# Attention, Fourier mixing and a feed-forward block in one kernel: instruction order from a table, and two PSUM tiles for the last product

## The chip, the cores and the metric

The kernel runs on one core of one Trainium2 chip. A core has TensorE (PE in the profile: matrix products, written to PSUM), VectorE (DVE), ScalarE (ACT), GpSimd (POOL) and SyncE (SP); each engine runs its own queue of instructions in the order in which they were put there, and waits on semaphores for the others. POOL and SP issue the transfers as well. The metric is the device time of one execution in microseconds (us); lower is better. Three executions of the kernel before took 565.71, 566.06 and 567.05 us, median 566.06.

## The reference

Inputs are `q`, `k`, `v` of (8, 12, 448, 64) and the weights `w_ch1` (768, 3072) and `w_ch2` (3072, 768); the output is (8, 448, 768), float32.

```python
scores = np.matmul(q, k.transpose(0, 1, 3, 2)) / np.sqrt(64)
attn = np.maximum(scores, 0.0) ** 2 / 448
x = np.matmul(attn, v).transpose(0, 2, 1, 3).reshape(8, 448, 768)
X = np.fft.fft(np.fft.fft(x, axis=1), axis=2)
u = x + np.real(X)
un = (u - mean(u)) / np.sqrt(var(u) + 1e-06)      # over the last axis
out = u + np.maximum(un @ w_ch1, 0.0) @ w_ch2
```

## The kernel before

Everything is bf16 on TensorE. The work is cut into pieces that are Python generators ("streams"); each `yield need(engine, duration, deps, bufs)` asks for one step on one engine, and emits the step's instructions when it is let on. `Streams.run` is a list scheduler that runs while the program is built: it keeps an estimated clock for each engine, and lets on the stream that can begin first, with small head starts by kind of stream and phase. So the order on every queue comes out of estimated durations. Nothing of this runs on the chip.

The streams, with the lines that show in the profile:

- **Loading** (POOL's queue, `load_group` L478, `load_halves` L453): q, k and v of one batch and four heads at a time. From batch 2 on DVE rearranges q and k (L585) and SP turns them by DMA (L595); batches 0 and 1 are turned on PE (L625).
- **Attention**: 21 items for each batch. An item's scores are two products (L956, PSUM tiles `psS`, three of them with two banks each, `BS`); ACT applies the relu (L969), which frees the PSUM tile, and DVE squares in place (L986; some squares are on ACT, L983). Six times a batch four squared items meet `v` (L824, L829, PSUM tile `psF`, two banks, `BF`), and the result leaves to `xT` (L691 on DVE, L688 on ACT).
- **Mixing**: `x` is folded by symmetry on DVE (L762 to L782), meets the channel table (L1434) and the sequence table (L1242, L1246); L1254 to L1259 take the two halves of PSUM apart. `mix_rows` adds `x` (L1277, L1279: one half of the rows on DVE, the other on POOL), takes the statistics (L1286, L1287 on DVE, root L1289 on ACT, L1291, L1292 on DVE), and normalises (L1305 on ACT or L1302 on POOL). `un` goes to DRAM (L1340, L1343) and comes back turned (L1382); batches 0 and 1 are turned on PE (L1132, L1207).
- **Feed-forward** over 12 groups of tokens, the last four of 256 tokens in two pairs. First products L1934 into `psF`, relu into `hT` on ACT (L1921) or DVE (L1919). The second products run as plain sums (L1962), or as two schemes that save products by sums of blocks: `whole` (L1989) and `Pair` (L2075). A scheme adds one PSUM tile to two blocks of the output, so that a product into a tile can go on only when DVE has added the tile as it is so far to its block `o` (L1625); then the tile goes on accumulating. In `joint`, the last two pairs, the first products are saved in the same manner: L1766, with copies of the running sums on ACT (L1781).
- **Output**: `o` starts as `u` from DRAM (L1597), and is stored when all its additions are in (L1605, SP's queue).
- **Warming** (L2158): 252-column products of zeros that fill PE's queue in the head of the program until the first batch's channel mixing is through.

`Pair.chain_a` is a tile's chain of four products: block by block it is added to `(c, 0)`, `(c+1, 0)`, `(c+1, 1)` and, complete, to `(c, 1)`. In the very last pair the fourth product is done in two halves of 192 columns, `parts`, both into the chain's own tile, so that the first half of the rows can be added and stored apart.

Of the kernel before, what the change touches and what calls it, by code (L numbers as in the profile page):

```python
# [41 lines left out]
class Banks(Bufs):  # L42
# [6 lines left out]
    def take(self, apart=None):  # L49
        first = min(self.ids)  # L50
        if apart is not None:
            held = {i // 2 for _, i in self.tiles.values() if i < 6}
            first = min(self.ids, key=lambda x: (x[0] > apart, x[1] // 2 in held, x))
        self.ids.remove(first)
        t = self.make(first[1])
        self.tiles[id(t)] = t, first[1]
        return t
# [7 lines left out]
HEAD = {('attentions', 'PE', 2): -0.6, ('attentions', 'PE', 3): -0.6, ('attentions', 'PE', 4): 0.07, ('mix_rows', 'PE', 2): -0.05}  # L65
# [3 lines left out]
PHASES = (48.0, 140.0, 290.0, 440.0)  # L69


class Streams:
# [29 lines left out]
    def run(self):  # L102
        end = {}
        while self.streams:
            for s in self.streams:
                if s[2] is None:
                    try:
                        s[2] = s[0].send(end.pop(id(s), None))
                    except StopIteration:
                        s[2] = ()  # L110
            self.streams = [s for s in self.streams if s[2] != ()]
            best = spare = None
            now = self.engine["PE"]
            phase = sum(now >= x for x in PHASES)
            for s in self.streams:
                eng, dur, deps, bufs, ok = s[2]
                if any(isinstance(d, Cell) and d.t is None for d in deps):
                    continue
                if any(len(p.free) < bufs.count(p) for p in bufs):
                    continue  # L120
                t = [self.engine[eng]] + [d.t if isinstance(d, Cell) else d for d in deps]
                for p in set(bufs):
                    t.append(sorted(p.free)[bufs.count(p) - 1])
# [3 lines left out]
                if key[0] and eng == "PE" and self.fill() and (spare is None or key < spare[0]):  # L127
                    spare = (key, s)
            if best is None:
                assert not self.streams, "stuck"  # L130
                break
            if best[1][2][0] == "PE" and spare is not None and best[0][1] - spare[0][1] > 0.5:
                best = spare
# [12 lines left out]
            end[id(s)] = start + dur  # L146
            s[2] = None

# [29 lines left out]
def kernel(  # L178
# [63 lines left out]
    STAGE[0] = 1  # L242
# [406 lines left out]
    def fold(b, m, F, av, give, av_end):  # L649
# [4 lines left out]
        def leave():  # L654
# [10 lines left out]
            if b == 0:  # L665
                bufs = [BX[m]] + ([BA[m]] if m < 3 else [])
                wait = {x: max(av_end, sch.engine[x]) + sch.queued(x) for x in ("ACT", "DVE")}
                en = "ACT" if m == MC - 1 or m in (3, 4) and wait["ACT"] + 2 * act(HS) < wait["DVE"] + 2 * dve(HS) else "DVE"
# [167 lines left out]
    def attention(b, left=None):  # L836
# [8 lines left out]
        while pv < MC:  # L845
            if p == NB and pv == MC - 1 and 2 <= b < B - 1 and turned_at[b + 1][0][0].t is not None:
                return F, sqs
            few = b == 0 or progress[0] == 0.0
# [15 lines left out]
            if values:  # L864
                deps += [sv[i][1] for i in items(mv)]
                if b > 1:
                    yield need("PE", 0.0, deps, [], gate)
                    if chains[0] == 2:
                        homes, n = BS, min(n, 2)
# [92 lines left out]
    def squares(b, scs, sqs):  # L962
        for i, sc, t in scs:
            e = yield need("ACT", act(2 * S) - (0.0 if STAGE[0] else 0.03), [t + LATENCY["PE"]], [BSQ])
            at = min(sq_ids)
            sq_ids.remove(at)
# [8 lines left out]
    def sooner(t, other, d, usual, du):  # L975

        wait = {en: max(t, sch.engine[en]) + sch.queued(en) for en in (other, usual)}
        return wait[other] + d + SPARE < wait[usual] + du
# [637 lines left out]
    def adder(b, NC, pool):  # L1616
# [4 lines left out]
        def add(pc, e, c, hf, give=True, cols=slice(0, DH)):  # L1621
# [4 lines left out]
            if give:  # L1626
                pool.give(pc, e)
            if cols.stop < DH:
# [393 lines left out]
    class Pair:  # L2022
# [79 lines left out]
        def chain_a(self):  # L2102
# [13 lines left out]
            t = yield from self.add(pc, e, c + 1, 1, False)  # L2116
            for cols in self.parts:
                n = cols.stop - cols.start
                e = yield need("PE", KP * mm(n), [t] + self.r4)
                self.product(pc, self.block(1, self.L), self.weights(1, 1), False, cols=cols)  # L2120
                self.done[0].t = e
                if n < DH:
                    sch.add(self.add(pc, e, c, 1, cols.stop == DH, cols), (0, 0))
# [95 lines left out]
```

## Time and profile before

| | us |
|---|---|
| median of three executions | 566.06 |
| the profiled execution | 566.29 |
| its span in the profile | 564.5 |
| PE busy | 555.8 |
| DVE busy | 437.5 |
| ACT busy | 319.8 |
| POOL busy | 196.3 |
| last PE instruction ends, from the span's start | 560.65 |

The span runs from the first to the last instruction of the profiled execution; 1.8 us lie outside it. Busy times of PE count each product to its modelled end, and products overlap: a product's start to the next one's start is shorter than its duration. A line of the timeline gives the start, the time until the group's end, the engine, the line of the program, the operation, the tile written and read, and the number of instructions; in brackets how long the engine sat idle before it, and on which instruction's end.

### The profile page before, as it was taken

To read this page: it belongs to the slowest core of one execution; us is meant where nothing else is said; L and a number is where in the kernel's file an instruction comes from. 1 tells how busy PE (TensorE), PEld (TensorE's weight loads), DVE (VectorE), ACT (ScalarE), POOL (GpSimd) and SP (SyncE) were. 2 spreads that over 40 slices of the span, in tenths; PEclk is the share of its full clock that TensorE was granted. 3 is DMA by queue.
4 is the path that set the end of the run, shared out by engine and by line. 5 is a ranking of instruction groups with operands and counts; after the bars stand their busy time and mean duration, and the time that the engine had idled before them with its cause. 6 is when DMAs were issued, how large, how long until landed. Compare 5 with 4: busy or idle time off the path is not lost.

```text
span 564.5 us, 11177 instructions
## 1 busy us (share of the span) xinstructions
PE 555.8 (98%) x4166; PEld 350.2 (62%) x4171; DVE 437.5 (77%) x1016; ACT 319.8 (57%) x536; POOL 196.3 (35%) x281
## 2 busy tenths in 40 slices
PE   8999999999999999999999999999999999999997
PEld 4375556544465455556756757767678688668864
DVE  7976565988789878887997897878899967555752
ACT  5978762676745686585786637638615264006400
POOL 8966215533346234462545545322005000000000
PEclk9999999999999999999999999999999999999999
DMA  9999999979968988899699979956425431332012
GB/s 115 177 208 240 209 213 169 259 102 135 179 99 208 201 132 178 163 185 206 155 166 177 220 123 189 168 128 154 116 66 161 120 93 21 79 109 74 2 58 83
DMA packets 152690, 82.43 MB, mean 146 GB/s; under 512 B 118076, under 2 KB 147900, under 8 KB 152636
## 3 DMA queue, kind: packets, MB, share of 16 engines
q0 software_dynamic: 57056, 33.63, 42.6%
q1 hardware_dynamic: 95580, 48.09, 37.9%
q8 instruction: 32, 0.52, 0.4%
q14 instruction: 22, 0.18, 0.1%
HBM read 62.91 MB, written 26.25 MB: 158 GB/s over the span
## 4 chain that ended last, share of the span: by engine, by line
PE 88%; DVE 4%; DMA 3%; ACT 2%; issue 1%; POOL 1%; DVEq 0%; POOLq 0%; ACTq 0%
PE psF L1934 26%; PE psF L2075 20%; PE psS L1766 8%; PE psS L956 8%; PE psS L2075 5%; PE psF L829 5%; PE psF L1989 4%; DMA kn<-in_k_dram 3%; PE psF L1766 2%; PE psS L1434 2%; PE psF L1962 2%; PE psF L824 1%; PE psF L625 1%; DVE sq L986 1%; PE psS L829 1%
## 5 line engine op out<-in xcount | busy, mean ns | idle before, releaser
L1934 PE MATMUL psF<-unT,w 128*128 128x256 bf16 (+2 forms) x1147 | 164.8, 299 | 0.3
L969 ACT ACTIVATE sq<-psS 128x896 bf16<-128x896 f32 x168 | 144.1, 920 | 31.5 <-PE psS L956 30.7
L1934 PEld LDWEIGHTS <-w 128*128 128x128 bf16 x1152 | 111.0, 98 | 49.7 <-issue 5.6
L986 DVE TENSOR_TENSOR sq<-sq 128x896 bf16<-128x896 bf16 x144 | 89.0, 635 | 13.2 <-ACT sq L969 12.2
L2075 PEld LDWEIGHTS <-hT 128*128 128x128 bf16 x648 | 62.5, 98 | 44.1 <-issue 4.8
L1921 ACT ACTIVATE hT<-psF 128x512 bf16<-128x512 f32 (+2 forms) x121 | 59.6, 508 | 41.1 <-PE psF L1934 40.0
L1625 DVE TENSOR_TENSOR o<-psF,o 128x384 f32<-128x384 f32 (+1 forms) x78 | 42.5, 547 | 24.5 <-PE psF L2075 20.1
L2075 PE MATMUL psF<-w,hT 128*128 128x384 bf16 x336 | 59.7, 326 | 0.6 <-DVE o L1625 0.6
L956 PE MATMUL psS<-qkT 64*128 64x448 bf16 (+1 forms) x336 | 51.5, 355 | 0.9 <-DVE qkT L632 0.8
L1781 ACT COPY copies<-psS 128x256 f32<-128x256 f32 x57 | 20.5, 372 | 47.2 <-PE psS L1766 47.2
L691 DVE TENSOR_SCALAR xT<-psF 128x224 bf16<-128x224 f32 x60 | 20.6, 384 | 26.3 <-PE psF L829 26.2
L1277 POOL TENSOR_TENSOR u<-tp,xn 112x385 f32<-112x385 f32 (+2 forms) x14 | 14.5, 1035 | 73.0 <-DVE tp L1257 49.1
L478 POOL DMA_DIRECT2D qn<-in_q_dram x21 | 15.7, 747 | 59.1 <-DVE qkr L585 52.9
L829 PE MATMUL psF<-sq,vn 128*64 128x448 bf16 x246 | 33.0, 362 | 0.0
L956 PEld LDWEIGHTS <-qkT 64*128 64x128 bf16 (+1 forms) x336 | 12.8, 94 | 32.3 <-issue 26.8
L1766 PEld LDWEIGHTS <-w 128*128 128x128 bf16 x288 | 28.2, 98 | 3.7
L453 POOL DMA_DIRECT2D kn<-in_k_dram x42 | 25.8, 624 | 11.5 <-PE psS L956 5.4
L1286 DVE BATCH_NORM_STATS2 stats<-u 112x6 f32<-112x384 f32 (+2 forms) x56 | 28.7, 543 | 1.0 <-POOL u L1277 0.7
L453 POOL DMA_DIRECT2D vn<-in_v_dram x42 | 26.1, 638 | 6.6 <-DMA w<-in_moe_w_ch_dram 5.8
L478 POOL DMA_DIRECT2D vn<-in_v_dram x24 | 18.9, 788 | 24.9 <-PE psS L956 24.7
L1305 ACT ACTIVATE un<-u,small 112x768 bf16<-112x768 f32 (+2 forms) x22 | 22.0, 1023 | 9.6 <-DVE small L1292 8.4
L829 PEld LDWEIGHTS <-vn 128*64 128x64 bf16 x288 | 12.5, 108 | 21.1 <-issue 17.5
(238 smaller groups left out, 950.5 us busy)
## 6 DMA issues: line engine op xcount, KB each, us to landing
out_dram<-o SPq DMA_DIRECT2D x55, 192.0 KB
qn<-in_q_dram POOLq DMA_DIRECT2D x21, 224.0 KB, 17.4
vn<-in_v_dram POOLq DMA_DIRECT2D x24, 192.0 KB, 5.0
w<-in_moe_w_ch_dram POOLq DMA_DIRECT2D x12, 384.0 KB, 9.5
w<-in_moe_w_ch_dram POOLq DMA_DIRECT2D x4, 1152.0 KB, 16.0
kn<-in_k_dram POOLq DMA_DIRECT2D x21, 192.0 KB, 5.7
utop<-u SPq DMA_DIRECT2D x12, 336.0 KB
o<-utop SPq DMA_DIRECT2D x16, 192.0 KB
```

The costliest lines, as they stand in the source:

```text
L453: nc.gpsimd.dma_start(out=t[par * Dh:(par + 1) * Dh, par::2], in_=at)
L478: nc.gpsimd.dma_start(out=to, in_=src[b, hs, 0:rows].rearrange("h (p j) d -> p h (j d)", j=j))
L829: nc.tensor.matmul(av[h * Dh:(h + 1) * Dh, 0:S], lhsT=vn_home[:, at:at + Dh], rhs=sq[:, h, :], start=start, stop=stop, skip_group_check=True)
L956: nc.tensor.matmul(sc[:, h, 0:S].rearrange("k (c q) -> k c q", c=4), lhsT=flat[ps, k0:k0 + KB], rhs=qT[ps, pair], start=True, stop=True)
L969: nc.scalar.activation(r, sc[:, :, 0:S], AF.Relu)
L986: nc.vector.tensor_tensor(r, r, r, op=ALU.mult)
L1286: nc.vector.bn_stats(stats[:n, hf, :], u[:n, hf * (D // 2):(hf + 1) * (D // 2)])
L1625: nc.vector.tensor_tensor(o[:, cols], pc[:, cols], o[:, cols], op=ALU.add)
L1766: nc.tensor.matmul(ps[:, 0:N], lhsT=lhs, rhs=rhs[:, m], start=(start and m == 0), stop=(stop and m == 2), skip_group_check=True)
L1921: nc.scalar.activation(hs, ps, AF.Relu)
L1934: nc.tensor.matmul(ph[:, i * N:(i + 1) * N], lhsT=w1_sb[m][hf][:, (jj + i) * 128:(jj + i + 1) * 128], rhs=unT[:, m, 0:N], start=(m == 0), ...
L2075: nc.tensor.matmul(pc[:, cols], lhsT=lhs[i], rhs=rhs[i][:, cols], start=(start and i == 0), stop=(i == KP - 1), skip_group_check=True)
```

## The change

The list scheduler's choice is replaced by a table. `ORDER` is a string of some 3,000 characters, one for each step: a character is the place, in the list of streams, of the stream whose step is next. It was found by a search outside of the program. Other decisions that hung on the estimated clocks (which PSUM tile or buffer is taken, whether an item's square goes to ACT or DVE, whether values and scores run together) go through `chosen`, which gives what the code would choose, or what the table `CHOICES` says for that question. The head, up to the first batch's channel mixing on PE, stands as before.

```diff
@@ Streams.run
-        while self.streams:
+        for code in ORDER:
...
-            best = spare = None
-            now = self.engine["PE"]
-            phase = sum(now >= x for x in PHASES)
-            for s in self.streams:
...
-                key = (ok is not None and not ok(), max(t) + HEAD.get((s[3], eng, phase), 0.0), s[1][eng != "PE"])
-                if best is None or key < best[0]:
-                    best = (key, s)
...
-            s = best[1]
+            s = self.streams[CODES.index(code)]
@@ the tables
+CODES = '0123456789ABCDEFGHIJKLMNOPQRSTUVWX'
+ORDER = "".join((
+    '009000000200999999999999999991111N1N029991999909919G102NN01991F111888MM4400F11L88L88884L088M84L1',
...
+CHOICES = {
+    78: 0, 80: 1, 94: True, 107: 0, 153: True, 155: False, 166: False, 170: True, 175: False,
...
+def chosen(x):
+    asked[0] += 1
+    return CHOICES.get(asked[0] - 1, x)
@@ adder
-        def add(pc, e, c, hf, give=True, cols=slice(0, DH)):
+        def add(pc, e, c, hf, give=True, cols=slice(0, DH), last=True):
...
+            if not last:
+                return
@@ Pair.chain_a
             t = yield from self.add(pc, e, c + 1, 1, False)
+            if len(self.parts) > 1:
+                sch.add(self.add(pc, e, c, 1, True, last=False), (0, 0))
             for cols in self.parts:
                 n = cols.stop - cols.start
-                e = yield need("PE", KP * mm(n), [t] + self.r4)
-                self.product(pc, self.block(1, self.L), self.weights(1, 1), False, cols=cols)
+                own = n < DH
+                e = yield need("PE", KP * mm(n), ([] if own else [t]) + self.r4, [self.pool] if own else [])
+                if own:
+                    pc = self.pool.take(e)
+                self.product(pc, self.block(1, self.L), self.weights(1, 1), own, cols=cols)
```

By operations the two programs are the same on ACT, POOL and SP: 538, 286 and 267 instructions each, of the same kinds and shapes. PE has two more products of zeros (L2158: 57 against 55, counting their weight loads). DVE has one more addition of 128x384 (L1625: 77 against 76), since the last chain's tile is added to `(c, 1)` before the two halves, which now have a PSUM tile each.

Three places of the order follow. Rows of the changed program carry its own line numbers, which are some 50 higher: L1004 is L956 of the kernel before, L1036 is L986, L1327 and L1329 are L1277 and L1279, L1393 is L1343, L478 and L453 have become L526 and L501, L1625 has become L1675, and L2075 has become L2127.

First, PE in the feed-forward group that it runs at about 258 us of the profile before, where a chain's tile (`psF_3410` before, `psF_3407` after) is added to its block and goes on with the next product, `w2_0` by `hT`. Before, that product follows the one before it in the same tile:

```order
L2075 LDWEIGHTS hT_886
L2075 MATMUL psF_3410<-w2_3_1064,hT_886 128x384
L2075 LDWEIGHTS hT_886
L2075 MATMUL psF_3410<-w2_0_979,hT_886 128x384
L2075 LDWEIGHTS hT_886
```

In the changed program the rows between the two, directly behind the last `w2_3` product into `psF_3407`, are:

```order
L1004 LDWEIGHTS qkT_3314
L1004 MATMUL psS_3594<-qkT_3314 128x448
L1004 LDWEIGHTS qkT_3314
L1004 MATMUL psS_3594<-qkT_3314 128x448
L1004 LDWEIGHTS qkT_3314
L1004 MATMUL psS_3597<-qkT_3314 128x448
L1004 LDWEIGHTS qkT_3314
L1004 MATMUL psS_3597<-qkT_3314 128x448
L2127 LDWEIGHTS hT_886
L2127 MATMUL psF_3407<-w2_0_1009,hT_886 128x384
```

Two more score products, of `psS_3591`, stand ahead of these. The three items' scores, which stood in front of the chain's `s1` product before, have moved in between the two products.

Second, POOL where batch 1's rows are mixed. Before, the additions of `x` (L1277, L1279) stand behind the loads of a later group of q and k:

```order
L478 DMA qn_1502<-in_q_dram 112x4x256
L478 DMA kn_122<-in_k_dram 128x4x192
L453 DMA kn_122<-in_k_dram 64x2x64
L1277 TENSOR_TENSOR u_1551<-tp_1527,xn_1043 128x385
L1279 TENSOR_TENSOR u_1551<-qs_1516,xn_1043 128x383
L1277 TENSOR_TENSOR u_1564<-tp_1538,xn_1043 112x385
L1279 TENSOR_TENSOR u_1564<-qs_1524,xn_1043 112x383
```

The changed program has, from the same load of q on:

```order
L526 DMA qn_1537<-in_q_dram 112x4x256
L1327 TENSOR_TENSOR u_1549<-tp_1539,xn_1209 128x385
L1329 TENSOR_TENSOR u_1549<-qs_1533,xn_1209 128x383
L1327 TENSOR_TENSOR u_1552<-tp_1529,xn_1209 112x385
L1329 TENSOR_TENSOR u_1552<-qs_1511,xn_1209 112x383
L526 DMA kn_122<-in_k_dram 128x4x192
L501 DMA kn_122<-in_k_dram 64x2x64
```

The four additions have moved ahead of two loads of k.

Third, DVE at the end of the program (`o_7420` is the last block of the output). Before:

```order
L1625 TENSOR_TENSOR o_6896<-psF_6266,o_6896 128x384
L1625 TENSOR_TENSOR o_6869<-psS_7406,o_6869 128x384
L1625 TENSOR_TENSOR o_6869<-psF_6266,o_6869 128x384
L1625 TENSOR_TENSOR o_6896<-psS_7406,o_6896 128x384
L1625 TENSOR_TENSOR o_7420<-psF_6266,o_7420 128x192 x2
```

The changed program:

```order
L1675 TENSOR_TENSOR o_6894<-psF_6252,o_6894 128x384
L2115 TENSOR_TENSOR hB_6192<-hB_6192,quarter_6154 128x2x128
L1675 TENSOR_TENSOR o_7368<-psS_7404,o_7368 128x384
L1675 TENSOR_TENSOR o_7420<-psF_6252,o_7420 128x384
L1675 TENSOR_TENSOR o_7420<-psS_7451,o_7420 128x192
L1675 TENSOR_TENSOR o_7420<-psS_7468,o_7420 128x192
```

The two halves come out of two tiles, `psS_7451` and `psS_7468`, and the chain's own tile is added to `o_7420` ahead of them; L2115 (L2063 before), the last of the operand that the two halves read, has moved behind the addition of `psF_6252`.

More of the change, by code (lines that the diff above doesn't have):

```diff
@@ L53, in take @@
             first = min(self.ids, key=lambda x: (x[0] > apart, x[1] // 2 in held, x))
+        w = chosen(first[1])
+        first = next((x for x in self.ids if x[1] == w), first)
         self.ids.remove(first)
@@ L147, in run @@
             s[2] = None
+        for s in self.streams:
+            assert s[2] is None and next(s[0], None) is None
 def need(eng, dur, deps=(), bufs=(), ok=None):
@@ L667, in leave @@
                 wait = {x: max(av_end, sch.engine[x]) + sch.queued(x) for x in ("ACT", "DVE")}
-                en = "ACT" if m == MC - 1 or m in (3, 4) and wait["ACT"] + 2 * act(HS) < wait["DVE"] + 2 * dve(HS) else "DVE"
+                en = "ACT" if chosen(m == MC - 1 or m in (3, 4) and wait["ACT"] + 2 * act(HS) < wait["DVE"] + 2 * dve(HS)) else "DVE"
                 for out_, in_ in (xa, xb):
@@ L845, in attention @@
         while pv < MC:
[L846 removed]
+            if p == NB and pv == MC - 1 and 2 <= b < B - 1 and chosen(turned_at[b + 1][0][0].t is not None):
                 return F, sqs
[L848 removed]
+            few = chosen(b == 0 or progress[0] == 0.0)
             n = min(1 if few else 3, NB - p)
@@ L965, in squares @@
             at = min(sq_ids)
+            w = chosen(at[1])
+            at = next((x for x in sq_ids if x[1] == w), at)
             sq_ids.remove(at)
@@ L977, in sooner @@
         wait = {en: max(t, sch.engine[en]) + sch.queued(en) for en in (other, usual)}
-        return wait[other] + d + SPARE < wait[usual] + du
+        return chosen(wait[other] + d + SPARE < wait[usual] + du)
     def square(b, r, t, done, scalar):
```

58 lines of the change are left out of this document (37 added, 21 removed), and 20 rows, old and new, of the table CHOICES.

## The prediction

> **What bounds the kernel now.** First the page's busy times and its chain of waits:
>
> ```profile
> PE 555.8 (98%) x4166; PEld 350.2 (62%) x4171; DVE 437.5 (77%) x1016; ACT 319.8 (57%) x536; POOL 196.3 (35%) x281
> PE 88%; DVE 4%; DMA 3%; ACT 2%; issue 1%; POOL 1%; DVEq 0%; POOLq 0%; ACTq 0%
> ```
>
> PE is busy for 98% of the span and makes up 88% of the chain that ended last. A change that leaves PE's products as they are can win only where PE stands still, and behind PE's last product. So the second view is the busy time by stretches (stretch; length, PE, PEld, DVE, ACT, POOL; clock, DMA), cut where PE loses time; the two stretches left out are the head up to 48 us and a full one from 262 to 290:
>
> ```profile
> 48.00:100.00 52.00, 51.93 (x380) 28.83 (x379) 32.28 (x74) 30.31 (x45) 21.08 (x31) 1.00 1.31 203
> 100.00:104.00 4.00, 3.68 (x32) 2.27 (x31) 3.86 (x14) 2.53 (x4) 3.81 (x6) 1.00 1.40 206
> 104.00:130.00 26.00, 25.69 (x155) 12.10 (x155) 22.36 (x52) 19.45 (x28) 7.77 (x11) 1.00 0.93 167
> 130.00:250.00 120.00, 119.84 (x763) 61.99 (x765) 100.87 (x239) 80.17 (x130) 53.15 (x70) 1.00 1.00 163
> 250.00:262.00 12.00, 11.35 (x84) 6.66 (x82) 9.06 (x19) 6.93 (x9) 2.50 (x4) 1.00 1.22 244
> ...
> 290.00:298.00 8.00, 7.79 (x50) 4.34 (x49) 7.86 (x23) 6.62 (x11) 3.88 (x4) 1.00 1.10 181
> 298.00:560.65 262.65, 262.65 (x2046) 188.50 (x2043) 197.15 (x449) 114.94 (x221) 50.78 (x58) 1.00 0.52 114
> 560.65:564.50 3.85, 0.00 (x1) 0.00 (x0) 0.62 (x2) 0.00 (x0) 0.00 (x0) 1.00 0.17 56
> ```
>
> Length less PE's busy time gives idle times of 0.07, 0.32, 0.31, 0.16, 0.65, 0.21 and 0 us: 1.72 us from 48 us to PE's end. A busy row ends with the last product's modelled end, which the next product would have overlapped, so each real stall is some 0.1 to 0.2 longer than its idle time. Behind PE lie 3.85 us in which DVE works for 0.62. Third, the list of PE's waits from 48 us on (us in total, times, longest):
>
> ```profile
> PE psF L2075 <- DVE o L1625: 0.9, 2, 0.6
> PE psS L1207 <- ACT un L1305: 0.3, 1, 0.3
> PE psF L824 <- ACT hT L1921: 0.2, 1, 0.2
> ```
>
> Four waits make up 1.4 of the 1.7 us, and none is for a transfer.
>
> **The change part by part.** All removed work is waiting; PE's products stay, but for two of zeros.
>
> *The wait for an addition at 258 us.* Timeline rows:
>
> ```profile
> 256.35 1.14 PE L2075 MATMUL psF<-w,hT 128*128 128x384 bf16 x6
> 257.52 0.56 DVE L1625 TENSOR_TENSOR o<-psF,o 128x384 f32<-128x384 f32 x1
> 258.14 2.11 PE L2075 MATMUL psF<-w,hT 128*128 128x384 bf16 x12 [0.65 <-DVE o L1625]
> ...
> 288.79 1.04 PE L956 MATMUL psS<-qkT 64*128 64x448 bf16 x6
> ```
>
> Twelve such products take 2.11 and six 1.14, so one takes (2.11 - 1.14)/6 = 0.16 of PE. The first six are through at 256.35 + 6 x 0.163 = 257.33, and the next starts at 258.14: the stall is **0.81 us**, namely the last product's end (0.16), the addition (0.56) and two hand-overs. By the order, six score products now stand between. Six of them took 1.04 at 288 us, less 0.16 for the last one's end 0.88, and the stall was 0.81. What is late next is L1434's input from L782 on DVE, whose step L780 now runs ahead of this addition, so earlier. I count the whole 0.81.
>
> *The wait for `un` at 102 us.*
>
> ```profile
> 97.19 0.60 POOL L453 DMA_DIRECT2D kn<-in_k_dram  x1
> 97.80 0.93 POOL L1277 TENSOR_TENSOR u<-tp,xn 128x385 f32<-128x385 f32 x1
> 100.71 1.30 PE L1962 MATMUL psF<-w,hT 128*128 128x384 bf16 x7
> 102.33 0.51 PE L1207 MATMUL psS<-ident,un 128*128 128x128 bf16 x6 [0.32 <-ACT un L1305]
> ```
>
> Seven products from 100.71 are through at 101.85; less 0.1 for an ordinary change of operands the stall is **0.38**. The addition of `x` on POOL starts as the issue of `kn` ends: it stood behind that queue, and behind it stand the statistics on DVE and `un` on ACT. The two issues that move behind the additions took about 0.6 each by that row, so the additions come some 1.2 us earlier against a need of 0.4. The moved loads come about 3.6 us later (four additions of 0.9); nothing on PE waits for a load after 48 us, so I cost that at nothing, and if that cover is gone, at what those 3.6 us leave of it (third rival).
>
> *The relu at 124 us and the addition at 295 us.*
>
> ```profile
> 121.61 1.72 ACT L969 ACTIVATE sq<-psS 128x896 bf16<-128x896 f32 x2
> 121.78 1.89 PE L1934 MATMUL psF<-unT,w 128*128 128x512 bf16 x8
> 123.20 0.62 ACT L1921 ACTIVATE hT<-psF 128x512 bf16<-128x512 f32 x1
> 123.88 0.35 PE L824 MATMUL psF<-sq,vn 128*128 128x448 bf16 x1 [0.20 <-ACT hT L1921]
> ...
> 293.86 1.01 DVE L1286 BATCH_NORM_STATS2 stats<-u 112x6 f32<-112x384 f32 x2
> 295.03 0.51 DVE L1625 TENSOR_TENSOR o<-psF,o 128x384 f32<-128x384 f32 x1
> 295.60 1.62 PE L2075 MATMUL psF<-hT 128*128 128x384 bf16 x9 [0.21 <-DVE o L1625]
> ```
>
> At 124 us the relu that frees `psF` ran behind two relus of scores (1.72 us); one of them now stands behind it, which gives 0.86 for a stall of 0.20 plus the overlapped 0.17, **0.37**. At 295 us the addition ran behind statistics of 1.01 us, and these behind an addition that itself waits for PE; that one now stands behind the needed one. The stall is 0.21 plus some 0.1, **0.29**. Both go.
>
> *Small waits.* What the stretches 48 to 100 and 130 to 250 lose (0.07 + 0.16), with as much again overlapped, is 0.4; the orders of relus there change. I count **0.3**.
>
> *The last product.*
>
> ```profile
> 558.51 2.14 PE L2075 MATMUL psF<-w,hB 128*128 128x192 bf16 x24
> 560.69 0.62 DVE L1625 TENSOR_TENSOR o<-psF,o 128x192 f32<-128x192 f32 x2 [1.42 <-PE psF L2075]
> 561.07 0.33 SPq L1605 DMA_DIRECT2D out_dram<-o  x1
> 561.50 0.38 SPq L1605 DMA_DIRECT2D out_dram<-o  x1
> ```
>
> Both halves of the addition wait for the 24th product, since both are in one tile. With a tile each, the first half can be added behind the 12th, 1.07 us earlier, and the whole addition of 0.56 that is new lies in DVE's 1.42 of idle time. Then only the second half, 0.31, stands behind PE, and the last store is issued where the first was, at 561.07: **0.43** less.
>
> *The head.*
>
> ```profile
> 31.44 0.38 PE L2158 MATMUL psS<-warm 128*128 128x252 bf16 x2
> 31.66 0.25 PE L1409 MATMUL psS<-chan,fold 128*128 128x193 bf16 x1
> ```
>
> Two zeros products take 0.22 from start to start, and two more stand ahead of L1409, which waits for nothing: **+0.22**, or nothing if what follows L1409 waits for another engine anyhow.
>
> *New waits.* Every queue is reordered, so some will come. Their nearest rows are in the last pairs (L1766), where copies of running sums lie on ACT:
>
> ```profile
> 464.59 0.49 PE L1766 MATMUL psS<-chan,w 128*128 128x256 bf16 x3
> 464.85 0.37 ACT L1781 COPY copies<-psS 128x256 f32<-128x256 f32 x1 [0.28 <-PE psS L1766]
> 464.92 0.27 PE L1766 MATMUL psS<-chan,quarter 128*128 128x256 bf16 x1
> ```
>
> A sum of three products takes 0.33 of PE (464.59 to 464.92). Before, a copy has at least three such sums as cover; in the changed order eleven copies have two, 0.66. The chain is a last product's 0.27 less the 0.11 that is PE's own time, the copy's 0.37, and two hand-overs of some 0.05: 0.63. They just fit; 0.1 short in each would be 1.1 us. Bounds of all new waits: 0 and 1.5 (these, and one more like that at 295 us); an estimate near the lower one, as each must outlast its cover, is **0.2**.
>
> Sum: -0.81 - 0.38 - 0.37 - 0.29 - 0.3 - 0.43 + 0.22 + 0.2 = **-2.16 us**, so 566.29 - 2.16 = 564.13 for the profiled execution. That one lay 0.23 above the median, 566.06; against the median it is **563.9**.
>
> **The rivals.** *First, slower: the copies in the last pairs.* ACT has no second queue: where a copy finds another one ahead of it, it starts a copy's 0.33 to 0.37 later, and PE, which has 0.03 to spare, waits for that, with the rest of the chain behind it. All eleven: +3.6, and 566.06 - 2.36 + 3.6 = **567.3**; with two ahead, near 571. It decides from eight copies on (8 x 0.33 = 2.6). For it: the changed order gives up a sum of cover. Against: ACT is idle 0.28 before a copy in the row above, and from 298 us on it is busy for 115 of 263 us. Chance 0.08.
>
> *Second: DVE and POOL get in each other's way.* The additions of `x` run on both:
>
> ```profile
> 101.40 0.56 DVE L1277 TENSOR_TENSOR u<-qs,xn 112x385 f32<-112x385 f32 x1
> 336.09 1.82 DVE L1277 TENSOR_TENSOR u<-qs,xn 112x385 f32<-112x385 f32 x1
> 336.50 0.93 POOL L1277 TENSOR_TENSOR u<-tp,xn 112x385 f32<-112x385 f32 x1
> ```
>
> The same addition on DVE takes 0.56 at 101 us and 1.82 where one of POOL falls into it: 1.26 more. The new order lets other pairs meet. Where one meets a chain's addition, PE sees what its cover leaves; the nearest row is the 0.29 at 295 us. Five of these: +1.5, and 566.06 - 2.36 + 1.5 = **565.2**. For it: the order of POOL's additions changes, as the second excerpt shows. Against: the 1.26 at 336 us cost PE nothing. The Trainium skill, "SBUF — State Buffer", section "Who interferes with whom", states that DVE and GpSimd share a port pair under an exclusive lock, so that of two that need it the second is blocked fully. The longer row agrees; by that rule alone each meeting costs DVE POOL's 0.93, so the sum would be 565.2 only if a third of each reached PE, and 568.4 if all of five did. Chance 0.22.
>
> *Third: the waits only move.* PE's engines that feed it are busy too: DVE for 7.86 of the 8.00 us around 295 us, for 3.86 of 4.00 at 102. If a product brought forward leaves its cover elsewhere, or a load of `kn` that is 3.6 us later is now missed, only tail and head are left: 566.06 - 0.43 + 0.22 = **565.85**. Chance 0.12.
>
> **How the numbers follow.** My forecast has 0.58, the rivals 0.08, 0.22 and 0.12. A measurement tells 0.3%, 1.7 us, from no change: faster is below 564.4, slower above 567.8. The forecast's own range is 563.2 (no new wait, none in the head, all small ones gone: -2.8) to 565.2 (1.5 of new waits); some nine tenths of it is faster, and a little of the second rival: 0.54. The third, most of the second and half of the first are within 0.3%: 0.40. Slower has the rest of the first, and meetings of DVE and POOL that all reach PE: 0.06. The range goes from 563.1 to 566.0, which takes in the second and third rival and leaves out the first.
>
> **What would show it.** PE's idle time from 48 us to its end falls from 1.7 to some 0.4 us, with no wait of 0.3 or more; L2075 at 258 us has no wait for `o`; L1207 none for `un`; behind PE's last product lie 3.4 us. The first rival shows as waits of L1766 for L1781; the second as additions on DVE of over 1 us with a wait of PE behind them; the third as waits of a like sum at other lines. Wrong in its base would be the prediction if PE's own busy time changed by more than the 0.2 of zeros.

## The result, and the profile after

Thirteen executions of each kernel, in turns:

| | before | changed |
|---|---|---|
| median, us | 566.32 | 570.13 |
| lowest to highest, us | 565.71 to 571.52 | 566.17 to 571.67 |
| executions of 569 us or more | 1 of 13 | 9 of 13 |
| ratio, 95% interval | | 1.0052 (1.0036 to 1.0069) |

The ratio, 1.0052, is the recorded one, as are all ratios below; it comes with its interval from all executions and isn't the quotient of the two medians. The changed kernel is slower by half a per cent, and its times fall into two groups: four of 566.2 to 567.7 and nine of 569.4 to 571.7. The profiled execution is one of the first group, 566.17, and there the kernel is level with the profile before (566.29). So two things have to be explained: why a short execution brings 0.1 us in place of 2.2, and what the other 4 us of a long one are.

The page's busy times of the changed kernel:

```profile
PE 556.2 (99%) x4173; PEld 350.7 (62%) x4173; DVE 429.5 (76%) x1017; ACT 316.1 (56%) x536; POOL 195.1 (35%) x281
```

Its busy time by the same stretches as before, in the same columns (the one from 262 to 290 had been left out there, with PE at 28.00 of 28.00 us):

```profile
100.00:104.00 4.00, 4.00 (x34) 2.60 (x32) 3.90 (x13) 3.25 (x5) 3.69 (x6) 1.00 1.15 218
104.00:130.00 26.00, 26.00 (x157) 12.29 (x156) 20.91 (x49) 18.92 (x27) 6.27 (x10) 1.00 0.85 149
130.00:250.00 120.00, 119.75 (x766) 62.03 (x765) 101.43 (x240) 79.19 (x129) 51.00 (x68) 1.00 1.05 160
250.00:262.00 12.00, 12.00 (x93) 7.47 (x91) 9.93 (x20) 7.73 (x9) 4.71 (x6) 1.00 1.18 253
262.00:290.00 28.00, 27.21 (x223) 18.15 (x221) 23.81 (x54) 20.86 (x32) 14.35 (x20) 1.00 0.97 149
290.00:298.00 8.00, 7.96 (x51) 4.45 (x50) 7.90 (x22) 5.69 (x10) 1.32 (x2) 1.00 0.87 115
298.00:560.65 262.65, 262.26 (x2042) 188.24 (x2040) 189.84 (x455) 112.48 (x222) 51.77 (x59) 1.00 0.55 117
560.65:564.40 3.75, 0.34 (x5) 0.11 (x2) 0.36 (x1) 0.00 (x0) 0.00 (x0) 1.00 0.42 143
```

The stretches around 102, 124 and 258 us are now full, and the one around 295 lost 0.04 in place of 0.21. But 130 to 250 lost 0.25, 262 to 290 lost 0.79, and 298 to 560 lost 0.39, where there was 0.16, nothing and nothing. PE's waits from 48 us on (in total, times, longest):

```profile
PE psF L1986 <- DVE xT L739: 0.8, 1, 0.8
PE psS L1004 <- DMA qkT<-qkr: 0.4, 1, 0.4
PE psF L2127 <- DVE o L1675: 0.2, 1, 0.2
```

These are three new waits, one for each of the three stretches. The timeline shows the first two to have a cause in common. At 241 us:

```profile
240.00 0.89 POOL L1329 TENSOR_TENSOR u<-qs,xn 112x383 f32<-112x383 f32 x1
240.32 2.13 DVE L1578 TENSOR_TENSOR hT<-w,wsum 128x1152 bf16<-128x1152 bf16 x1
240.84 1.01 POOL L1352 TENSOR_SCALAR un<-u,small 112x768 bf16<-112x768 f32 x1
242.38 0.55 DVE L1675 TENSOR_TENSOR o<-psF,o 128x384 f32<-128x384 f32 x1
242.98 0.81 PE L2127 MATMUL psF<-w,hT 128*128 128x384 bf16 x4 [0.25 <-DVE o L1675]
```

and at 270 us:

```profile
269.52 1.68 DVE L1329 TENSOR_TENSOR u<-tp,xn 113x383 f32<-113x383 f32 x1
269.93 0.85 POOL L1329 TENSOR_TENSOR u<-qs,xn 113x383 f32<-113x383 f32 x1
271.60 0.67 DVE L739 TENSOR_SCALAR xT<-psF 128x224 bf16<-128x224 f32 x2
272.32 0.94 PE L1986 MATMUL psF<-unT,w 128*128 128x256 bf16 x7 [0.79 <-DVE xT L739]
```

Sums of that form on DVE (L1578 with 1152 columns, L1329) take 0.75 and 0.55 us where POOL has no instruction beside them; with two of POOL in the first and one in the second they took 2.13 and 1.68. What PE waits for, an addition to `o` and the copy that frees a PSUM tile, stands behind them in DVE's queue. By starts of products the two stalls are 0.41 and 0.95 us. This is my second rival. The third wait is for a transfer that turns a group of q and k, issued by SP 7.5 us earlier:

```profile
305.08 1.70 SPq L643 DMA_TRANSPOSE qkT<-qkr  x1
312.69 0.55 PE L1004 MATMUL psS<-qkT 64*128 64x448 bf16 x4 [0.35 <-DMA qkT<-qkr]
```

### The profile page after: what moved, and what is told of

It is laid out like the page before. It is cut to its first block, busy times and chain, and to the rows that moved or that the text cites. A ratio compares the mean times of both kernels' runs of the same rounds, so it can differ in the third digit from the quotient of the medians.

```text
span 564.4 us, 11127 instructions
## 1 busy us (share of the span) xinstructions
PE 556.2 (99%) x4173; PEld 350.7 (62%) x4173; DVE 429.5 (76%) x1017; ACT 316.1 (56%) x536; POOL 195.1 (35%) x281
## 4 chain that ended last, share of the span: by engine, by line
PE 93%; DVE 3%; DMA 1%; issue 1%; ACT 1%; POOL 0%; DVEq 0%; POOLq 0%
PE psF L1986 27%; PE psF L2127 21%; PE psS L1004 8%; PE psS L1818 8%; PE psS L2127 6%; PE psF L877 5%; PE psF L2014 4%; PE psF L2041 4%; PE psF L1818 2%; PE psS L1484 2%; DMA qkT<-qkr 1%; PE psF L872 1%; PE psF L673 1%; PE psS L877 1%; PE psS L1459 1%
## 5 line engine op out<-in xcount | busy, mean ns | idle before, releaser
L1019 ACT ACTIVATE sq<-psS 128x896 bf16<-128x896 f32 x168 | 145.7, 919 | 39.2 <-PE psS L1004 38.9
L1036 DVE TENSOR_TENSOR sq<-sq 128x896 bf16<-128x896 bf16 x144 | 87.7, 631 | 15.7 <-ACT sq L1019 15.1
L2127 PEld LDWEIGHTS <-hT 128*128 128x128 bf16 x648 | 62.4, 98 | 44.0 <-issue 4.2
L1675 DVE TENSOR_TENSOR o<-psF,o 128x384 f32<-128x384 f32 x77 | 42.3, 550 | 24.2 <-PE psF L2127 17.9
L2127 PE MATMUL psF<-w,hT 128*128 128x384 bf16 x336 | 60.1, 326 | 0.2 <-DVE o L1675 0.2
L1004 PE MATMUL psS<-qkT 64*128 64x448 bf16 (+1 forms) x336 | 51.6, 355 | 1.2 <-DVE qkT L680 0.7
L1327 POOL TENSOR_TENSOR u<-tp,xn 112x385 f32<-112x385 f32 (+2 forms) x14 | 14.2, 1012 | 67.6 <-DVE tp L1307 33.3
L739 DVE TENSOR_SCALAR xT<-psF 128x224 bf16<-128x224 f32 x60 | 21.8, 385 | 19.9 <-PE psF L877 19.8
L1004 PEld LDWEIGHTS <-qkT 64*128 64x128 bf16 (+1 forms) x336 | 13.0, 94 | 32.5 <-issue 26.2
L526 POOL DMA_DIRECT2D kn<-in_k_dram x21 | 16.2, 774 | 39.9 <-DVE qkr L633 26.6
L526 POOL DMA_DIRECT2D qn<-in_q_dram x21 | 15.5, 740 | 40.3 <-DVE qkr L633 25.0
L501 POOL DMA_DIRECT2D kn<-in_k_dram x42 | 26.0, 629 | 8.3 <-PE psS L1004 5.0
L501 POOL DMA_DIRECT2D vn<-in_v_dram x42 | 26.7, 645 | 3.6 <-DMA w<-in_moe_w_ch_dram 3.4
L1971 DVE TENSOR_SCALAR hT<-psF 128x512 bf16<-128x512 f32 (+3 forms) x35 | 17.9, 528 | 13.1 <-PE psF L1986 12.9
L1393 POOL DMA_INDIRECT nbot<-un,backs x12 | 12.7, 1056 | 41.2 <-ACT un L1355 39.8
```

What stands on the lines that cost most here:

```text
L501: nc.gpsimd.dma_start(out=t[par * Dh:(par + 1) * Dh, par::2], in_=at)
L526: nc.gpsimd.dma_start(out=to, in_=src[b, hs, 0:rows].rearrange("h (p j) d -> p h (j d)", j=j))
L1004: nc.tensor.matmul(sc[:, h, 0:S].rearrange("k (c q) -> k c q", c=4), lhsT=flat[ps, k0:k0 + KB], rhs=qT[ps, pair], start=True, stop=True)
L1019: nc.scalar.activation(r, sc[:, :, 0:S], AF.Relu)
L1036: nc.vector.tensor_tensor(r, r, r, op=ALU.mult)
L1675: nc.vector.tensor_tensor(o[:, cols], pc[:, cols], o[:, cols], op=ALU.add)
```

## The experiments

All kernels that follow keep the computation whole. But for `tail`, which is a change of the code, and `mixed`, which joins the two orders, each moves a few steps in a table of the changed kernel's form, so that the rest of every queue stays in its order.

### What a long execution is: the changed kernel twice more

> The changed kernel once more, unchanged, for the profile of one of its longer executions (of 13, four took 566.2 to 567.7 us, nine took 569.4 to 571.7 with a mean granted clock of 0.996 to 0.999). Theory A, a late transfer: in a long execution PE stands still for 2 us or more behind one transfer (or behind an instruction that waits for one) at a place where the short profile has no wait, and the granted clock falls for about 3 us right after it. Theory B, the clock by itself: the clock falls with no longer wait ahead of it; then 0.003 x 569 us at half speed explain 1.7 of the 4.3 us, and the rest lies in many small waits. Theory C, VectorE and GpSimd in each other's way: several additions of over 1 us on DVE, each with a wait of PE of up to 1 us behind it, spread over the middle of the program.

> The same kernel a second time, in case that the first execution is a short one. Each theory expects what it expects of the first: A one place with a wait of 2 us or more, the same place in each long execution; B none; C several waits below 1 us.

Both came out long, 570.61 and 568.99 us. The first one's timeline, SP and then PE:

```profile
305.98 2.39 SPq L643 DMA_TRANSPOSE qkT<-qkr  x1
...
315.07 0.55 PE L1004 MATMUL psS<-qkT 64*128 64x448 bf16 x4 [2.72 <-DMA qkT<-qkr]
```

Its busy time by stretches, with PE's clock behind the engines' columns:

```profile
312.30:315.73 3.43, 0.71 (x8) 0.28 (x7) 1.65 (x4) 1.17 (x2) 0.74 (x1) 1.00 1.63 254
315.73:319.14 3.41, 3.41 (x18) 2.44 (x17) 0.94 (x3) 1.47 (x2) 0.00 (x0) 0.50 1.14 133
```

The same two views of the second one:

```profile
315.25 0.55 PE L1004 MATMUL psS<-qkT 64*128 64x448 bf16 x4 [2.92 <-DMA qkT<-qkr]
```

```profile
310.37:313.78 3.41, 1.97 (x17) 0.91 (x14) 3.27 (x7) 1.88 (x3) 0.74 (x1) 1.00 1.35 117
313.78:317.20 3.42, 1.95 (x18) 1.44 (x19) 0.23 (x1) 1.54 (x2) 0.00 (x0) 1.00 1.41 223
```

It is theory A: the wait for the turning transfer, 0.35 in the short execution, is 2.7 and 2.9 us in the long ones. In the first, PE's clock then falls to half for 3.41 us, which costs 1.7 us with PE busy throughout; 2.4 of longer wait and 1.7 are 4.1 of the 4.4 us; behind PE's last product lie 3.79 us in place of 3.39, which is the rest. In the second, with the longer wait, the clock doesn't fall, and that execution is 1.6 us shorter.

### The last product alone

> The kernel before, with its own order, and only the two PSUM tiles of the last product and the addition that goes with them. If the tail is worth what the prediction says: 0.4 us less (ratio 0.9992), PE ends where it did and the span ends 3.4 us behind PE instead of 3.85. If the two tiles had a part in the long executions: some of its times at 570 or above. If they belong to the order alone: times like those of the kernel before, 565.3 to 567, with a long one as rare as there (1 of 13).

Median 566.11 against 567.13 of the kernel before beside it (17 executions), ratio 0.9983 (0.9970 to 0.9996), highest 568.11. Behind PE's last product lie 3.39 us, as in the changed kernel, in place of 3.86. The long executions don't come from it. (Its edit is the part of the change's diff on `adder` and `chain_a`.) Its profile, of an execution of 568.11, shows one thing that makes the old order vary:

```profile
PE psS L1207 <- ACT un L1305: 1.7, 1, 1.7
```

This is the wait at 102 us, 0.3 in the profile before. On POOL's queue loads wait for earlier ones to land. Here the run of loads began 0.7 us later and two such waits took 3.8 in place of 3.0 us, so that the additions of `x` behind them came 1.3 us later. The rest of this execution's length lies outside its span: 568.11 less 565.4 is 2.7 us, where it was 1.8 in the profile before. In the executions of the kernel before that ran beside the experiments this part is 1.7 to 3.0 us; in all 13 of the changed kernel it is 1.7 or 1.8. Why it varies is open.

### The transfer at 312 us: two single moves

```diff
 SP's queue (turn)
 L643 DMA_TRANSPOSE qkT_4207<-qkr_4082 128x8x112
 L1647 DMA o_4209<-ubot2_82 64x384
...
+L643 DMA_TRANSPOSE qkT_4207<-qkr_4205 128x8x128
...
 L1390 DMA utop4_76<-u_4006 112x768
-L643 DMA_TRANSPOSE qkT_4207<-qkr_4205 128x8x128
 POOL's queue (loads)
 L526 DMA qn<-in_q_dram 112x4x256
+L526 DMA kn<-in_k_dram 128x4x192
+L501 DMA kn<-in_k_dram 64x2x64 x2
+L526 DMA vn<-in_v_dram 128x4x192
+L501 DMA vn<-in_v_dram 64x2x64 x2
 L1393 DMA nbot<-un,backs
-L526 DMA kn<-in_k_dram 128x4x192
-L501 DMA kn<-in_k_dram 64x2x64 x2
-L526 DMA vn<-in_v_dram 128x4x192
-L501 DMA vn<-in_v_dram 64x2x64 x2
```

> The changed kernel with one step moved: on SP's queue the second turning transfer of the group of q and k that PE needs at 312 us (L643, qkT from qkr, kn's part) stands four places earlier, ahead of two transfers of xn and the stores of un and u; the other queues are as they were. Theory L (it is issued too late, 305.1 to 306.0 us in place of about 301.4 when its input is there): it lands before 310, PE's wait for it (0.35 in the short execution, 2.7 and 2.9 in the two long ones) goes, and with it every long execution: times of 565.5 to 567, median about 565.7, clock 1.000, ratio to the kernel before 0.998 to 1.000. Theory D (the shared DMA engines are full between 300 and 315 us whatever the order): the earlier transfer lands at 312 or later all the same, and about two in three executions stay above 569. Theory K (the clock falls by itself and the transfer is a bystander): no wait for qkT, but times above 569 with a clock of 0.997 go on.

> The changed kernel with another single move: on POOL's queue the loads of the next kn and vn (six issues) stand ahead of the scatter to nbot, which waits 2.85 us for un, as they do in the kernel before; SP's queue is as it was, so that the turning transfer is issued at 305 to 306 us as in the changed kernel. If the loads' bytes are what holds it up (theory S: in the changed kernel they are issued at 304.5 to 308.5 and share the DMA engines with the turning transfer; before, they were issued from 299.2 to 304.5): they are issued from 301.4 on, the transfer lands by 311.5, no wait of PE, no long execution, median about 565.7. If only the place on SP's queue matters (theory L alone): waits of 0.3 to 2.9 us as in the changed kernel, long executions in about two of three. If delayed scatters are what follows: a new wait for unT or for nbot behind 313 us.

Medians 566.91 (566.13 to 570.12) and 566.28 (565.66 to 568.11), against 566.78 of the kernel before; ratios 1.0002 (0.9987 to 1.0017) and 0.9996 (0.9983 to 1.0010). Of 12 executions each, one and none are above 569, where the changed kernel had 10 of 15. So the transfer is the cause of most of the long executions, and each move by itself is enough against it. That of `loads` says more: the transfer is issued even later, and yet is there in time.

```profile
306.93 2.51 SPq L643 DMA_TRANSPOSE qkT<-qkr  x1
...
313.08 0.82 PE L1004 MATMUL psS<-qkT 64*128 64x448 bf16 x6
```

PE's six products run through, so it had landed by 313.5, 6.5 us after its issue; in the changed kernel it took 7.5 in the short execution and 9.1 in the long one. There the loads of `kn` and `vn` are issued behind POOL's scatter to `nbot` (L1393, which puts rows of `un` in DRAM), from 304.5 to 308.5 us, within 0.6 us ahead of the transfer's issue and 3.4 us behind it; here all of them are issued ahead of it, from 302.7 to 306.7. That their packets hold the transfer up is the reading that fits both moves; packet by packet it wasn't followed.

Neither median came down to the 565.7 expected, since other waits took the place. In `turn`, PE's list shows two waits for `o`, of 0.9 us, one of them new at 330 us: DVE stands still on the next turning transfer, and two instructions stand between the one that waits and the addition that PE needs.

```profile
328.73 0.43 DVE L633 COPY qkr<-qn 112x1024 bf16<-112x1024 bf16 x1 [1.75 <-DMA qkT<-qkr]
...
330.42 1.14 PE L2127 MATMUL psF<-wsum,s 128*128 128x384 bf16 x6 [0.61 <-DVE o L1675]
```

In the profile of `loads` the new one is at 198 us, 100 us ahead of the move, so it was luck of that execution and no effect of it:

```profile
PE psF L1986 <- DMA unT<-nbot: 0.8, 1, 0.8
```

### POOL and DVE at 270 and 241 us

```diff
 POOL's queue (lock272)
 L526 DMA kn<-in_k_dram 128x4x192
+L501 DMA kn<-in_k_dram 64x2x64 x2
 L1329 TENSOR_TENSOR u<-qs,xn 113x383
-L501 DMA kn<-in_k_dram 64x2x64 x2
 POOL's queue (three and best, besides)
+L501 DMA vn<-in_v_dram 64x2x64 x2
 L1352 TENSOR_SCALAR un<-u,small 112x768
-L501 DMA vn<-in_v_dram 64x2x64 x2
```

> The changed kernel with two issues of loads of kn (1.2 us) moved ahead of one addition of x on POOL (L1329 at 269.9 us), so that it doesn't run while DVE does its own L1329 (269.5 us, which took 1.68 in place of 0.55). Theory V (the two additions block each other, and the copy of xT that frees PE's tile stands behind on DVE): DVE's L1329 takes 0.55 to 0.6, the copy L739 ends 1.1 us earlier, and PE's wait of 0.8 for it at 272.3 us goes (0.95 by starts of products). Theory Q (DVE is full at this place, the long addition is no cause): the wait stays above 0.5. The time itself says little in one execution: 565.2 in a short one.

```profile
270.68 0.55 DVE L1329 TENSOR_TENSOR u<-tp,xn 113x383 f32<-113x383 f32 x1
271.22 2.02 PE L1986 MATMUL psF<-unT,w 128*128 128x256 bf16 x17
```

Theory V, in this execution: DVE's addition is back at 0.55 us and PE runs through. The place lies 1.1 us later here, after a wait of 0.75 us at 265 us, for another turning transfer, that the other profiles don't have. That execution was the longest of all, 572.98 us, with 3.2 us of wait at 312 and two stretches of 3.41 us at half clock behind it.

> The changed kernel with three moves: the turning transfer earlier on SP (as in turn), POOL's loads of kn ahead of the addition at 269.9 us (as in lock272), and on POOL two loads of vn ahead of the normalisation L1352 at 240.8 us, which ran into DVE's L1578 (2.13 in place of 0.75 us) ahead of an addition that PE waits for (0.25; 0.41 by starts). If the three new waits are what keeps the changed kernel from the gain that I forecast: 0.5 + 0.95 + 0.41 less than its short executions, that is 566.2 - 1.9 = 564.3 in all executions, ratio to the kernel before 0.995 to 0.997, and no wait of PE above 0.3 us between 60 and 560 us. If the moves open new waits elsewhere: 565 to 566, with these waits to be seen. If the long executions have another cause: some of its times stay above 569.

> The changed kernel with three moves: POOL's loads of kn and vn ahead of the scatter to nbot (as in loads), and the two moves that take POOL's work out of the way of DVE at 241 and 270 us (as in three). SP's queue stays. If these three places are the new waits, and each is gone without a successor: 566.2 - 0.5 - 0.95 - 0.41 = 564.3 in a short execution, none above 569. If the waits only move along: 565.3 to 567.5 with waits of 0.3 to 0.9 at other lines, as in turn (0.77 at 330 us) and in loads (0.9 at 198 us).

`three` has a median of 566.81 (565.50 to 571.62), ratio 0.9999 (0.9978 to 1.0020): worse than expected, with waits of 0.7 each for a relu on DVE and for `o` at 327 and 332 us, where DVE again stood still on a turning transfer, as in `turn`, and three of 12 executions above 569. The profile is of one of these, 569.01, and has no wait for the transfer at 312 us, so long executions have other causes too. `best` (the move of `loads` and the two on this side) has 566.03 (565.23 to 567.76), ratio 0.9991 (0.9977 to 1.0004), none above 569. Its profile, of 565.26, has one wait left of the three:

```profile
PE psF L1986 <- DVE xT L739: 0.3, 1, 0.3
```

So its short executions gain 0.9 of the 1.9 us expected: of the stall at 272 us half stayed (0.47 by starts), and small ones of up to 0.2 came. DVE's addition ahead of it took 1.19 us, with POOL's addition gone from it and only POOL's issues of loads beside it:

```profile
269.55 1.19 DVE L1329 TENSOR_TENSOR u<-tp,xn 113x383 f32<-113x383 f32 x1
269.92 1.21 POOL L501 DMA_DIRECT2D kn<-in_k_dram  x2
```

In `three` it took 1.19 too, in `lock272`, with the same neighbours, 0.55. So the meeting of the two additions is 1.68 - 1.19 = 0.5 us of it in these two runs, and what held DVE for the rest is open. In the kernel before the same addition (L1279, at 270.1 us) took 1.19 as well, and PE lost nothing: there DVE's chain lay some 0.5 us earlier against PE's products, and two products of L1242 stood in between. By these rows half of this stall comes from the new order's smaller cover, and not from a new meeting.

### The forecast's terms, in the old order

> The kernel before in its own order, with the two tiles of the last product, and one move on POOL: the four additions of x of batch 1 ahead of two loads of kn, as the changed kernel has them. In the profile of tail the additions ran 1.3 us later than in that of before, since a load ahead of them on POOL's queue had waited longer, and PE's wait for un at 104 us was 1.79 in place of 0.38. If that queue is what makes the kernel before vary between 565.7 and 568.5: no wait for un, and times of 564.9 to 566 only, ratio about 0.997. If the variation has other causes: the wait is gone, and the times still spread over 3 us.

> The kernel before in its own order with the two tiles and just the moves that answer to the four waits of my prediction, each made by itself: at 102 us POOL's additions ahead of two loads; at 258 us three items' scores on PE between the chain's two products, with DVE's order as it must be for that; at 124 us ACT's relu ahead of one relu of scores; at 295 us DVE's addition ahead of one statistics instruction. If the four terms are worth what the prediction says (0.38 + 0.81 + 0.37 + 0.29, and 0.43 of the tail): 566.1 - 2.3 = 563.8 in short executions and no wait of PE above 0.3 us behind 60 us, ratio 0.994 to 0.997. If a wait that is removed always brings another one: 565 to 566, with these waits to be seen near the four places.

> As four, but without its move on POOL at 102 us: the kernel before in its own order, the two tiles, and the moves at 258, 124 and 295 us. In the profile of four (a long execution) three additions of x on POOL ran into DVE's own (3.05 in place of 0.55 us), an addition that PE waits for stood behind it, PE waited 2.3 us and the clock fell for 3.4 us. If that meeting came from the move on POOL: no execution above 568.5, short ones at 564.3 (0.38 above those of four), and the spread of 1 to 2 us of the kernel before, whose additions keep their place. If it comes from loads that land late whatever the order: some executions above 569 here too.

> The changed kernel's order for the first 853 steps (to 146 us, where both orders have done nearly the same steps), then what is left in the order of the kernel before, with the moves at 258 and 295 us; the two tiles. In the changed kernel POOL's loads ahead of the additions at 95 us come 4 us earlier than in the kernel before, and its profiles show no wait at 102 or 124 us. If the early part of the new order is sound and its harm lies in the places at 243, 272 and 312 us alone: 563.7 to 564.8 in nearly all executions, no wait of PE above 0.3 us behind 60 us, ratio 0.995 to 0.997. If the early part has late transfers of its own: executions of 566 and above with a wait at 48 to 146 us.

| kernel | median | lowest to highest | ratio to before, 95% interval |
|---|---|---|---|
| tail102 | 566.77 | 565.26 to 571.42 | 1.0005 (0.9983 to 1.0027) |
| four | 565.34 | 563.89 to 569.47 | 0.9981 (0.9964 to 0.9997) |
| trio | 564.80 | 563.89 to 566.07 | 0.9960 (0.9944 to 0.9975) |
| mixed | 564.40 | 564.17 to 566.77 | 0.9966 (0.9954 to 0.9978) |

The kernel before beside them had 566.83 and 566.68. The edit that `four` and `trio` share, in the order's rows:

```diff
 PE (258 us), six score products moved down
-L1004 MATMUL psS<-qkT 128x448   (six, ahead of w_0 by s_2069)
...
 L2127 MATMUL psF<-w_3_1064,hT 128x384
+L1004 MATMUL psS<-qkT 128x448   (six)
 L2127 MATMUL psF<-w_0_979,hT 128x384
 DVE (258 us): the two squares of those scores move down behind L830
 ACT (124 us)
+L1973 ACTIVATE hT<-psF 128x2x256
 L1019 ACTIVATE sq<-psS 128x896
-L1973 ACTIVATE hT<-psF 128x2x256
 DVE (295 us)
 L1336 BN_STATS stats<-u 112x6
+L1675 TENSOR_TENSOR o<-psF,o 128x384
 L1336 BN_STATS stats<-u 112x6
 L1337 BN_AGGR small<-stats 112x2
-L1675 TENSOR_TENSOR o<-psF,o 128x384
```

`trio` beats both kernels: the waits at 258, 124 and 295 us are gone and nothing came in their place. By the prediction's terms these three and the tail are worth 0.81 + 0.37 + 0.29 + 0.43 = 1.9 us; the medians are 1.88 apart. PE's waits in its profile, of 564.44, are this one row:

```profile
PE psS L1257 <- ACT un L1355: 0.4, 1, 0.4
```

`mixed`, the new order up to 146 us and the old one with two moves behind it, has no row in that list at all, and 10 of its 12 executions lie between 564.17 and 565.04. So the new order does no harm up to 146 us; its harm lies behind.

`four` is as short as forecast in half its executions (563.89 to 564.80), and above 567.8 in three. Its profile is of a long one, 569.47, and shows the second rival at its dearest. From its timeline DVE, POOL's first and last of four additions, and PE:

```profile
98.60 3.05 DVE L1329 TENSOR_TENSOR u<-tp,xn 128x383 f32<-128x383 f32 x1
98.59 0.98 POOL L1327 TENSOR_TENSOR u<-tp,xn 128x385 f32<-128x385 f32 x1
...
101.13 1.21 POOL L1329 TENSOR_TENSOR u<-qs,xn 112x383 f32<-112x383 f32 x1
102.17 4.03 PE L2014 MATMUL psF<-w,hT 128*128 128x384 bf16 x14 [2.30 <-DVE o L1675]
```

and two stretches of its busy time:

```profile
98.60:102.03 3.43, 1.27 (x8) 0.66 (x7) 3.43 (x3) 0.00 (x0) 3.43 (x5) 1.00 1.46 181
102.03:105.44 3.41, 3.27 (x11) 1.54 (x11) 3.27 (x13) 0.89 (x3) 3.10 (x5) 0.50 1.09 279
```

POOL's additions, moved ahead of two loads, meet DVE's own when the loads in front of them land late; 0.55 us become 3.05, the addition behind it makes PE wait 2.3 us, and the clock falls. `trio`, which differs by this one move, has no such execution. And in `tail102` the same move alone doesn't take the wait for `un` away (0.4 in its profile): the additions start 1.5 us earlier than in `tail`, but DVE's own took 0.94 and 1.26 us beside them. In the changed kernel, and in `mixed`, the wait is gone. There POOL's whole run of loads is issued 4 us earlier, from 83.7 us in place of 88.0, and in the changed kernel POOL then waits 2.85 us for DVE and not for a load. That this is the reason fits the rows; no run moved these loads alone.

## Why the prediction was wrong

The step that failed is the term **new waits**: 0.2 us, "near the lower one, as each must outlast its cover", with bounds of 0 and 1.5. In the short execution they are 0.41 + 0.95 + 0.43 (0.52 less the 0.09 that products of this form have anyway) = 1.8 us, above the upper bound, and in a long one another 2.4 us of wait and 1.7 of halved clock, past every bound and rival that I gave but the dearest case of the first one (near 571), which didn't come.

- **The waits that go** were right: the stalls of 0.81, 0.38 and 0.37 are gone, that of 0.29 is 0.12. `trio` shows three of them to be real gains without the new order. At 102 us the reason was incomplete: the move of the additions ahead of two loads, which I counted on, alone brought nothing (`tail102`) or harm (`four`), and what goes with the gain in the changed kernel is the earlier issue of all loads ahead of them. (The two issues that moved took 1.57 us, from 96.23 to 97.80, and not 1.2: I read both from the shorter one's row.)
- **Tail and head** were right: 3.86 us behind PE's end became 3.39 (0.47 for 0.43; in the two longer executions it is 3.79 and 3.66), and the same product of the first weights starts at 57.10 in place of 56.91 us.
- **Small waits**: the idle times of PE below 0.15 us, from 48 us on, add up to 0.33 before and 0.15 in the changed kernel. That is 0.18, and 0.36 with as much again overlapped, as the prediction counts them, for 0.3.
- With the measured 1.8 and 0.36 the sum is about 0.6 below the profile before; measured is 0.1. The last 0.5 are not attributed. (The prediction's own lower end, -2.8, was 0.1 too low: its terms without new waits and head, and all small ones gone, give -2.68.)
- **The place that I bounded the new waits by was the wrong one.** The copies in the last pairs, eleven of them with 0.03 us to spare, cost nothing: no wait of PE stands behind 354 us. My first rival didn't come.
- **The second rival came, and dearer.** DVE and POOL met in places that PE feels: stalls of 0.41 and 0.95 us at two meetings, where I took 0.29 each; of the second, `best` shows half to come from the order around it. On the rule of the Trainium skill, "SBUF — State Buffer", section "Who interferes with whom", that the second of the two is blocked fully, the runs agree and go further: with four additions of POOL in a row, DVE's was held for 2.5 us, through three of them. The new order has fewer such meetings, at worse places: of DVE's 28 additions of `x`, nine took 0.9 us or more in the profile before, and four in that of the changed kernel.
- **The transfers I cost at nothing.** "Nothing on PE waits for a load after 48 us" was true of one profile. I read a margin from it, and none of the spread: in the old order the turning transfer at 312 us was issued at 305.7 and was in time; in the new one it was issued at 305.1, with POOL's loads moved beside it, and lands from 312.6 to 315.2.

## What to carry to other kernels

A profile shows one draw of the transfers' times: where an order is packed tighter, a wait that isn't there in one execution can be 3 us in the next, so margins to transfers need the spread of several profiles, and two kernels need more executions than a steady one would. When a wait is removed by moving work, move only what that wait needs: three waits and the tail, changed by hand in the old order, gave the 1.9 us that a reordering of everything gave back elsewhere. Where two engines share a resource, ask who stands behind the blocked instruction, and not how many microseconds of blocking there are in all.

## What was not expected of the hardware

PE's clock falls to half in steps of 3.41 us after a wait of 2.3 to 3.2 us. The records cut time into stretches of this length, at an offset that changes with each execution (a border lies at 315.73 us in `again1` and at 313.78 in `again2`). In `again1` PE was busy for 21% of the stretch ahead (0.71 of 3.43), in `four` for 37% (1.27 of 3.43), and the next stretch ran at half clock; in `again2` the longest wait of the three, 2.9 us, fell across a border, PE was busy for 58% and 57% of the two stretches (1.97 and 1.95 of 3.4), and the clock stayed. So the price of one and the same wait is 2.9 or 2.7 + 1.7 us, by where it falls.

Two more rows narrow it down, the stretches at 312 us in `lock272`, and the one in which PE's work ends in `mixed`, with what is left of its span:

```profile
311.17:314.58 3.41, 1.37 (x11) 0.37 (x9) 2.91 (x6) 1.51 (x2) 0.75 (x1) 1.00 1.45 138
314.58:318.00 3.42, 2.31 (x11) 1.18 (x12) 0.00 (x0) 1.71 (x2) 0.00 (x0) 0.50 1.18 237
...
557.58:560.99 3.41, 1.50 (x19) 1.27 (x16) 0.82 (x3) 0.00 (x0) 0.00 (x0) 1.00 0.34 115
560.99:562.46 1.47, 0.00 (x0) 0.00 (x0) 0.00 (x0) 0.00 (x0) 0.00 (x0) 1.00 0.00 0
```

After 40% (1.37 of 3.41) the clock fell, after 44% (1.50 of 3.41) it stayed. In `lock272` the first stretch at half clock was busy for 68% (2.31 of 3.42) and a second one followed, though in `again2` 57% were enough to stay at full; what it takes to get back is open. That the busy share of the stretch decides fits these rows; nothing was run to test it. The Trainium skill, "TensorE: Matmul & The Clock Gate", section "HAM oscillation — how this bites in real kernels", names idle gaps of more than about 3.4 us as what brings the clock down; here less was enough, and the measurement decides.
